# A state-space and MLP block on one core: group 1 turned by VectorE and transfers, not by TensorE

## The chip, the cores and the metric

The kernel runs on one core of a Trainium2 chip. The metric is the device time of one execution in microseconds; lower is better. The engines are named as in the profile: PE (TensorE; PEld is its weight load), DVE (VectorE), ACT (ScalarE), POOL (GpSimd), SP (SyncE, which here only issues transfers).

## The reference

All data is float32. The input `x` has 2048 tokens of 512 channels. A layer norm and a long convolution per channel (a state-space filter of 128 modes) give `h`; then a mixer and an MLP follow:

```python
h = x + conv(_layernorm(x))
z = _layernorm(h)
a = _gelu(_layernorm(z) @ w1)          # layer 1, 512 -> 512
hs = shifted(a) @ w2                   # layer 2: quarters of the channels shifted by +1, -1, +2, -2 tokens
x1 = z + hs
out = h + x1 + _gelu(_layernorm(x1) @ w3) @ w4   # layers 3 and 4, 512 -> 1792 -> 512
```

## The kernel before

`conv_phase` computes `h` under a planner that orders its operations by cost and due time. `mixer_phase` follows; there the order on each engine is that in which the Python code calls the operations (the class `InOrder` keeps it for PE, DVE, ACT and POOL). SP takes its transfers in program order too, and a transfer that waits holds back those behind it.

The tokens are kept as 16 tiles of 128, `h[:, j, :]`, in four groups of four tiles: group q has tiles 4q to 4q+3. The mixer takes group 3 first, then 0, 1 and 2. A matrix product is made of three products of float32r parts (`PROD`): high by high, high by low, low by high. So each operand is split into a high part (a copy on ACT) and a low part (a subtraction on DVE).

What happens to a group ahead of layer 1:

- `finish(q)`: bn_stats and bn_aggr of its tiles on DVE, in `conv_phase`. It can be called for some tiles at a time (`early` is the first two, `late` the other two).
- `root([q])`: twelve small DVE operations on the group's means and variances, which give the scale and the offset.
- `norm1(q)`, line 1214: the normalized tiles are written to a quarter each of a buffer `XQ[...]` (group 1 to `XQ[2]`), by DVE (tensor_scalar) or by ACT (activation), after the condition in line 1218.
- the turn, which brings channels onto the partitions. There are two ways. `turn1(q)` (line 1224) calls `transposed`: 16 TensorE transposes against `ident` into four PSUM banks, and `split` makes the high and low parts from there. `swap` (line 1227) takes four DVE transposes, each of one tile in 32x32 blocks, into a second buffer, and then 16 transfers of 32 partitions by 2 KB that carry the blocks back to where they belong; `parts` makes the high and low parts from the buffer. Each transfer reads blocks that all four transposes wrote. `swap` can be given an order of the tiles and a list of queues, which the transfers take in turn by `b`.

Before the change, groups 3, 0 and 1 go by `turn1` and group 2 by `swap` on SP's queue. The swaps of the later layer norm (`turn2`) use SP's queue, one of them SP's and ACT's.

`layer1(q, f)` (line 1246) makes one of four blocks of 128 outputs for a group: 12 matmuls into a PSUM bank out of four, then two gelus on ACT, a subtraction on DVE, and for some tiles the wrap copies on POOL, which layer 2 needs at the ends of the sequence. For (3, 0) the 12 products are re-sorted, so that high parts come first. `layer2(j)` makes one tile: 12 matmuls into a bank of the same four, then DVE adds (`scalar_tensor_tensor`), and for the first eight tiles POOL adds it to `h` (`residual`) and DVE takes its statistics. The order around the change is written out by hand in lines 1422 to 1431. `raw3`, `raw4` load weights on SP's queue, and `sum3` adds some of them on POOL.

The functions that the change touches, and what calls them:

Of the kernel before, what the change touches and what calls it, by code (L numbers as in the profile page):

```python
# [292 lines left out]
def norms(nc, cst, qs):  # L293

    ra, rb, rr, nb = cst["norm"]
    mv, t = cst["mv"], slice(qs[0] * 4, qs[-1] * 4 + 4)
    return [
        lambda: nc.vector.tensor_scalar(ra[:, 0, t], mv[:, t, 1], EPS, None, ALU.add),
        lambda: nc.vector.tensor_scalar(ra[:, 1, t], mv[:, t, 1], 1.0 + EPS, EPS * EPS, ALU.mult, ALU.add),
        *rsqrt_ops(nc, None, None, rr[:, :, t], ra[:, :, t], rb[:, :, t]),  # L300
        lambda: nc.vector.scalar_tensor_tensor(
            nb[:, :, t], mv[:, t, 0].unsqueeze(1).to_broadcast([128, 2, len(qs) * 4]), -1.0, rr[:, :, t], ALU.mult, ALU.mult),
    ]
# [825 lines left out]
def mixer_phase(ctx, tc, cst, h, out, finish, w3, w4):  # L1129

    nc = InOrder(tc)
# [10 lines left out]
    def slab(name):  # L1142
        return sl.tile([128, 512], F32R, tag="slab", name=name)
# [7 lines left out]
    XQ = [w1p.tile([128, 4 * 512], F32, name=f"xq{i}") for i in range(4)]  # L1151
# [5 lines left out]
    def bank(name):  # L1157
        return ps.tile([128, 512], F32, tag="bank", name=name)
# [11 lines left out]
    def gelu(b, name):  # L1170

        hi, lo, g = slab(f"{name}h"), slab(f"{name}l"), tmp(f"g{name}")
        nc.scalar.activation(hi, b, AF.Gelu_apprx_tanh)
        nc.scalar.activation(g, b, AF.Gelu_apprx_tanh)
        nc.vector.tensor_tensor(lo, g, hi.bitcast(F32), ALU.subtract)
        return hi, lo
# [10 lines left out]
    def root(qs):  # L1187
        for op in norms(nc, cst, qs):
            op()

    def transposed(tiles, name, first=0):

        b = [wide_bank(c, f"{name}_{c}") for c in range(4)]

        def turn(i, c):
            nc.tensor.transpose(b[c][:, i * 128 : i * 128 + 128], tiles[i][:, c * 128 : c * 128 + 128], ident)

        for i in range(first):  # L1200
            for c in range(4):
                turn(i, c)
        res = []
        for c in range(4):
            for i in range(first, 4):
                turn(i, c)
            res.append(split(b[c], f"{name}{c}"))
        return res
# [3 lines left out]
    H1, XL, XT = {}, {}, {}  # L1212

    def norm1(q):
        XL[q] = []
        for j in range(q * 4, q * 4 + 4):
            t = quarter(XQ[{3: 0, 0: 1, 1: 2, 2: 0}[q]], j % 4)
            if (q == 0 and j % 2) or (q == 3 and j != 14):
                nc.vector.tensor_scalar(t, h[:, j, :], mv[:, j, 0:1], r12[:, j : j + 1], ALU.subtract, ALU.mult)
            else:  # L1220
                nc.scalar.activation(t, h[:, j, :], AF.Identity, scale=r12[:, j : j + 1], bias=off12[:, j : j + 1])
            XL[q].append(t)

    def turn1(q):
        XT[q] = transposed(XL.pop(q), f"xt{q}", 2 if q == 3 else 0)

    def swap(x, t, order=range(4), queues=(nc.sync,), between=lambda: None):

        blocks = t.rearrange("p (b c i t) -> p i c b t", b=4, c=4, i=4)
        for i in order:  # L1230
            nc.vector.transpose(blocks[:, i], quarter(x, i).rearrange("p (c b t) -> p c b t", c=4, b=4))
        between()
        for a in range(4):
            for b in range(4):
                queues[b % len(queues)].dma_start(quarter(x, a)[b * 32 : b * 32 + 32], quarter(t, b)[a * 32 : a * 32 + 32])
        return [turned(x)[:, c] for c in range(4)]

    def parts(src, name, low=nc.vector):

        hi, lo = slab(f"{name}h"), slab(f"{name}l")  # L1240
        src = src.rearrange("p a (i t) -> p i a t", i=4)
        nc.scalar.copy(natural(hi), src)
        low.tensor_tensor(natural(lo), src, natural(hi).bitcast(F32), ALU.subtract)
        return hi, lo

    def layer1(q, f):
        b = bank(f"l1_{q}_{f}")
        n = 0
        seq = [(c, wi, xi) for c in range(4) for wi, xi in PROD]
        if (q, f) == (3, 0):  # L1250

            seq.sort(key=lambda k: 2 * k[0] + 3 * k[2])
        for c, wi, xi in seq:
            nc.tensor.matmul(b, W1[f][wi][:, c * 128 : c * 128 + 128], XT[q][c][xi], start=(n == 0), stop=(n == 11))
            n += 1
        H1[q, f] = gelu(b, f"h1_{q}_{f}")

        tiles = {0: ((15, 0),), 2: ((14, 1), (15, 2)), 1: ((0, 3),), 3: ((0, 4), (1, 5))}[f]
        for t, i in tiles:
            if t // 4 != q:  # L1260
                continue
            for k in range(2):
                src = H1[q, f][k][:, t % 4 * 128 : t % 4 * 128 + 128]
                dst = wrap[k][i // 4][:, i % 4, :]
                if f in (0, 2):
                    nc.gpsimd.tensor_copy(dst[:, 32:128], src[:, 0:96].bitcast(F32))
                    nc.gpsimd.tensor_copy(dst[:, 1:32], src[:, 96:127].bitcast(F32))
                    nc.gpsimd.tensor_copy(dst[:, 0:1], zero)
                else:
                    nc.gpsimd.tensor_copy(dst[:, 0:96], src[:, 32:128].bitcast(F32))  # L1270
                    nc.gpsimd.tensor_copy(dst[:, 96:127], src[:, 1:32].bitcast(F32))
                    nc.gpsimd.tensor_copy(dst[:, 127:128], zero)
# [3 lines left out]
    def h1_block(f, j, k):  # L1276
        if 0 <= j < 16:
            return H1[j // 4, f][k][:, j % 4 * 128 : j % 4 * 128 + 128]
        return wrap[k][WRAP[f, j] // 4][:, WRAP[f, j] % 4, :]
# [4 lines left out]
    def layer2(j):  # L1284
        q, i = divmod(j, 4)
        b = bank(f"l2_{j}")
        n = 0
        for f, sh in enumerate((-1, 1, -2, 2)):
            for wi, xi in PROD:
                nc.tensor.matmul(b, h1_block(f, j + sh, xi), W2[f][wi], start=(n == 0), stop=(n == 11))  # L1290
                n += 1
        x1 = quarter(X1[q], i)
        nc.vector.scalar_tensor_tensor(x1, h[:, j, :], r1[:, j : j + 1], b, ALU.mult, ALU.add)
        xq[j] = x1
        if j < 8:
            residual(j), stats2(j)

    def residual(j):
        (nc.gpsimd if j < 12 else nc.vector).tensor_tensor(h[:, j, :], h[:, j, :], xq[j], ALU.add)

    def stats2(j):
        q, i = divmod(j, 4)
        if q not in mv2:
            mv2[q] = sm.tile([128, 4, 2], F32, tag="mv2", name=f"mv2_{q}")
        st = sm.tile([128, 6], F32, tag="bst", name=f"st1_{j}")
        nc.vector.bn_stats(st, xq[j])
        nc.vector.bn_aggr(mv2[q][:, i, :], st)
# [62 lines left out]
    def raw3(s):  # L1370
        f = s % half
        for i in range(2):
            o = (f + i * half) * 128
            nc.sync.dma_start(raw["ab"[i]].rearrange("p (c f) -> p c f", c=4),
                              w3[:, o : o + 128].rearrange("(c p) f -> p c f", p=128))

    def sum3():
        a11, a12, a21, a22 = (raw[n][:, i * 256 : i * 256 + 256] for n in "ab" for i in range(2))
        s1, s2, s3, s4 = (raw["s"][:, i * 256 : i * 256 + 256] for i in range(4))
        nc.gpsimd.tensor_tensor(s1, a21, a22, ALU.add)  # L1380
        nc.gpsimd.tensor_tensor(s3, a11, a21, ALU.subtract)
        nc.gpsimd.tensor_tensor(s2, s1, a11, ALU.subtract)
        nc.gpsimd.tensor_tensor(s4, a12, s2, ALU.subtract)
# [16 lines left out]
    def raw4(s):  # L1400
        for i in range(2):
            f = s % half + i * half
            nc.sync.dma_start(raw["45"[i]], w4[f * 128 : f * 128 + 128, :])
# [15 lines left out]

    gelus = lambda: nc.scalar.activation(zero, zero, AF.Gelu_apprx_tanh)  # L1420
    early, late = range(2), range(2, 4)
    norm1(3), finish(0, early), turn1(3), gelus(), finish(0, late), root([0]), norm1(0)
    layer1(3, 0), layer1(3, 1), layer1(3, 2), turn1(0), finish(1), root([1]), layer1(3, 3), norm1(1), raw3(0), raw4(0)
    finish(2, early), layer1(0, 0), layer1(0, 1), layer1(0, 2), layer1(0, 3), turn1(1), finish(2, late), root([2]), layer2(0), layer2(1)
    norm1(2), sum3()
    third = swap(XQ[0], XQ[1])
    layer1(1, 0), layer1(1, 1), layer1(1, 2), layer1(1, 3), load3(0), raw3(1)
# [123 lines left out]
    for s in range(2 * half):  # L1551
# [27 lines left out]
        late = layer3b(s)  # L1579
# [56 lines left out]
```

## Time and profile before

| | us |
|---|---|
| median of 3 runs | 690.6 |
| lowest and highest run | 689.83, 692.06 |
| the profiled execution | 690.04 |
| its span, first to last instruction | 688.0 |
| PE busy | 651.1 |
| DVE, ACT, POOL busy | 543.0, 409.3, 398.5 |

A line of the timeline gives the start in us from the span's start, the length, the engine, the line of the code, the operation, the tile written and those read, the shapes and the count; in brackets stands how long the engine was idle before it and whose work ended that. Operations that follow one another overlap a little, so a cost is read from one start to the next. `SPq` and `ACTq` are the issues of transfers on those queues. A line of the chain of waits has start, length and what it is; every instruction is at line 87, the helper that keeps the order, so that the tiles' names tell them apart: `xt` are the turned inputs (xt10h: group 1, first 128 channels, high part), `l` the banks of layers 1 and 2, `h_0l` a low part of layer 1's output, `xq` the buffers.

### The profile page before, as it was taken

To read this page: it belongs to the slowest core of one execution; us is meant where nothing else is said; L and a number is where in the kernel's file an instruction comes from. 1 tells how busy PE (TensorE), PEld (TensorE's weight loads), DVE (VectorE), ACT (ScalarE), POOL (GpSimd) and SP (SyncE) were. 2 spreads that over 40 slices of the span, in tenths; PEclk is the share of its full clock that TensorE was granted. 3 is DMA by queue.
4 is the path that set the end of the run, shared out by engine and by line. 5 is a ranking of instruction groups with operands and counts; after the bars stand their busy time and mean duration, and the time that the engine had idled before them with its cause. 6 is when DMAs were issued, how large, how long until landed. Compare 5 with 4: busy or idle time off the path is not lost.

```text
span 688.0 us, 16756 instructions
## 1 busy us (share of the span) xinstructions
PE 651.1 (95%) x6822; PEld 507.7 (74%) x6822; DVE 543.0 (79%) x954; ACT 409.3 (59%) x708; POOL 398.5 (58%) x406
## 2 busy tenths in 40 slices
PE   5887989998999997989999999999999999999997
PEld 5884756663677684748888888888888888888886
DVE  5998898999898998988868799766879954454554
ACT  7889778867889975245734455544465543444330
POOL 1889589967999998002456209355635555554210
PEclk9998999999999999999999999999999999999999
DMA  8830644011201133010032311133311342211004
GB/s 216 258 145 2 194 153 104 3 48 32 64 3 50 33 111 93 2 61 1 1 92 74 82 30 38 55 90 99 104 46 40 103 132 62 62 46 47 18 13 123
DMA packets 48752, 50.43 MB, mean 73 GB/s; under 512 B 6180, under 2 KB 32804, under 8 KB 48676
## 3 DMA queue, kind: packets, MB, share of 16 engines
q1 hardware_dynamic: 47524, 47.80, 24.5%
q10 hardware_dynamic: 1152, 1.57, 0.9%
q8 instruction: 53, 0.87, 0.5%
q14 instruction: 23, 0.19, 0.1%
HBM read 35.72 MB, written 8.39 MB: 64 GB/s over the span
## 4 chain that ended last, share of the span: by engine, by line
PE 62%; DVE 14%; ACT 11%; POOL 4%; DMA 4%; issue 3%; SPq 1%; DVEq 0%; ACTq 0%; POOLq 0%
PE l L87 24%; PE acc L87 11%; PE bank L87 7%; ACT pt L87 7%; DVE u L87 4%; DVE at L87 3%; PE l3e L87 3%; PE l3c L87 3%; PE l3g L87 3%; PE l3f L87 3%; PE l3b L87 3%; PE l3a L87 3%; PE l3d L87 3%; DMA h<-in_A_u_dram 3%; DVE cs L87 2%
## 5 line engine op out<-in xcount | busy, mean ns | idle before, releaser
L87 ACT ACTIVATE pt<-pt 128x1056 f32<-128x1056 int32 x64 | 70.0, 1094 | 14.6 <-DVE cs L87 6.6
L87 POOL TENSOR_TENSOR pt<-p,s 128x512 int32<-128x512 int32 x64 | 72.2, 1146 | 4.5 <-DVE sn L87 3.6
L87 PE MATMUL bank<-at,tbs 128*64 128x128 f32 (+1 forms) x768 | 63.1, 311 | 3.4 <-DVE u L87 1.6
L87 PEld LDWEIGHTS bank<-at,tbs 128*64 128x64 f32 x768 | 44.6, 134 | 20.6 <-ACT at L87 2.9
L87 PEld LDWEIGHTS bank<-ident 128*128 128x128 f32 x418 | 49.9, 196 | 8.3 <-issue 5.1
L87 PE MATMUL bank<-ident 128*128 128x128 f32 x418 | 54.0, 285 | 0.0
L87 PE MATMUL bank<-u,ms 64*128 64x128 f32 x768 | 50.5, 280 | 3.5 <-DVE at L87 1.3
L87 PEld LDWEIGHTS bank<-u,ms 64*128 64x128 f32 x768 | 45.3, 187 | 8.3 <-issue 1.8
L87 POOL TENSOR_TENSOR cs0w<-raw,cs0w 128x512 fp32r<-128x512 f32 x7 | 9.1, 1297 | 58.9 <-ACT cs0w L87 47.3
L87 DVE TENSOR_TENSOR cs<-pt,amx 128x512 f32<-128x512 f32 x64 | 41.1, 682 | 2.4 <-ACT pt L87 1.2
L87 PEld LDWEIGHTS bank<-cs 128*32 128x32 f32 x1024 | 24.1, 111 | 22.5 <-POOL cs L87 6.0
L87 PE MATMUL bank<-cs 128*32 128x64 f32 x1024 | 32.4, 224 | 8.6 <-DVE cs L87 4.4
L87 DVE TENSOR_TENSOR h<-h,l 128x512 f32<-128x512 f32 x48 | 32.0, 685 | 10.6 <-PE l L87 10.6
L87 POOL TENSOR_TENSOR sn1w<-raw,sn1w 128x512 fp32r<-128x512 f32 x7 | 9.5, 1363 | 53.3 <-ACT sn1w L87 50.5
L87 ACT COPY at<-bank 128x512 f32<-128x512 f32 x40 | 24.9, 630 | 23.2 <-PE bank L87 23.1
L87 DVE TENSOR_TENSOR u<-u,l3f 128x512 f32<-128x512 f32 x14 | 9.6, 682 | 36.9 <-PE l3f L87 36.9
L87 ACT ACTIVATE pt<-pt,halfpi 128x1056 f32<-128x1056 f32 x32 | 38.2, 1192 | 0.5
L87 POOL TENSOR_TENSOR sn<-pt,amp 128x512 f32<-128x512 f32 x30 | 36.7, 1222 | 1.4 <-ACT pt L87 1.0
L87 DVE STREAM_TRANSPOSE at<-bank 128x512 f32<-128x512 f32 (+1 forms) x40 | 35.8, 930 | 1.9 <-PE bank L87 1.9
L87 ACT ACTIVATE u<-u 128x512 f32<-128x512 f32 x56 | 35.4, 633 | 1.8
L87 PE MATMUL bank<-sn 128*32 128x64 f32 x1024 | 31.9, 222 | 2.7 <-DVE sn L87 2.4
L87 POOL TENSOR_TENSOR cs<-pt,amp 128x512 f32<-128x512 f32 x26 | 31.8, 1223 | 3.6 <-PE bank L87 1.2
(1160 smaller groups left out, 2077.6 us busy)
## 6 DMA issues: line engine op xcount, KB each, us to landing
raw<-in_B_w_dram SPq DMA_DIRECT2D x28, 256.0 KB, 2.8
xq<-xq SPq DMA_DIRECT2D x72, 64.0 KB, 2.0
h<-in_A_u_dram SPq DMA_DIRECT2D x32, 128.0 KB, 4.2
h<-in_A_u_dram SPq DMA_DIRECT2D x16, 256.0 KB, 4.1
rawa<-in_B_w_dram SPq DMA_DIRECT2D x14, 256.0 KB, 2.8
rawb<-in_B_w_dram SPq DMA_DIRECT2D x14, 256.0 KB, 2.8
ms<-in_mm_dram SPq DMA_DIRECT2D x4, 768.0 KB, 11.2
out_dram<-h SPq DMA_DIRECT2D x48, 64.0 KB, 1.7
```

The source lines that it names most:

```text
L87: ins = f(*args, **kw)
```

## The change

Group 1 (tiles 4 to 7) is turned by `swap`, with its tiles in the order 1, 3, 0, 2 and its 16 transfers alternately on SP's queue and on GpSimd's; `turn1(1)` goes. `parts` of the result stands where `turn1(1)` stood. The first half of group 1's statistics moves ahead of layer 1 of group 3. `layer1(3, 3)` moves behind the normalization and the swap of group 1. In `norm1(1)`, two of the four tiles go to DVE. `layer1(1, 0)` takes its products in the re-sorted order.

```diff
-            if (q == 0 and j % 2) or (q == 3 and j != 14):
+            if (q < 2 and j % 2) or (q == 3 and j != 14):
...
-        if (q, f) == (3, 0):
+        if (q, f) in ((3, 0), (1, 0)):
...
-    norm1(3), finish(0, early), turn1(3), gelus(), finish(0, late), root([0]), norm1(0)
-    layer1(3, 0), layer1(3, 1), layer1(3, 2), turn1(0), finish(1), root([1]), layer1(3, 3), norm1(1), raw3(0), raw4(0)
-    finish(2, early), layer1(0, 0), layer1(0, 1), layer1(0, 2), layer1(0, 3), turn1(1), finish(2, late), root([2]), layer2(0), layer2(1)
+    norm1(3), finish(0, early), turn1(3), gelus(), finish(0, late), root([0]), norm1(0), finish(1, early)
+    layer1(3, 0), layer1(3, 1), layer1(3, 2), turn1(0), finish(1, late), root([1]), norm1(1), raw3(0), raw4(0)
+    second = swap(XQ[2], XQ[1], (1, 3, 0, 2), (nc.sync, nc.gpsimd))
+    layer1(3, 3), finish(2, early), layer1(0, 0), layer1(0, 1), layer1(0, 2), layer1(0, 3), finish(2, late)
+    XT[1] = [parts(v, f"xt1{c}") for c, v in enumerate(second)]
+    root([2]), layer2(0), layer2(1)
     norm1(2), sum3()
     third = swap(XQ[0], XQ[1])
```

## The prediction

> **What bounds the kernel now.** I read the page first (busy times, then the chain that ended last), then the chain in order of time, then each engine's timeline around the edit. On the page PE is busy for 95% of the span and carries most of the chain:
>
> ```profile
> PE 651.1 (95%) x6822; PEld 507.7 (74%) x6822; DVE 543.0 (79%) x954; ACT 409.3 (59%) x708; POOL 398.5 (58%) x406
> PE 62%; DVE 14%; ACT 11%; POOL 4%; DMA 4%; issue 3%; SPq 1%; DVEq 0%; ACTq 0%; POOLq 0%
> ```
>
> That is an average over stages, so the chain in order of time says more (start, length, what):
>
> ```profile
> 304.50 1.30 PE xt L87 x10
> 306.52 8.60 PE l L87 x36
> 315.12 1.75 PE xt L87 x16
> 316.87 13.65 PE l L87 x60
> 330.52 1.75 PE xt L87 x16
> 332.26 65.52 PE l L87 x288
> ```
>
> From 306.5 us on there are only PE pieces, end to end: the mixer is bound by PE, and every other engine hides behind it. The three "xt" pieces are the TensorE turns of groups 3, 0 and 1. The third is what the change takes out. So a gain can only be that piece, and a loss can only be PE made to wait.
>
> **What goes: PE's turn of group 1.**
>
> ```profile
> 330.13 0.39 PE L87 MATMUL l<-xt03h,sn0w 128*128 128x512 f32 x1
> 330.36 1.91 PE L87 MATMUL xt<-ident,xq 128*128 128x128 f32 x16
> 332.02 0.71 PE L87 MATMUL l<-sn0w,wrap 128*128 128x512 f32 x2
> 337.56 0.39 PE L87 MATMUL l<-xt10h,cs0w 128*128 128x512 f32 x1
> ```
>
> By starts, 332.02 - 330.36 = **1.66 us** leave PE. Then layer2(0) follows layer1(0,3) directly and needs its low part ten matmuls later. The trace has this meeting already, at layer1(1,3) and layer2(2):
>
> ```profile
> 348.21 0.39 PE L87 MATMUL l<-xt13h,sn0w 128*128 128x512 f32 x1
> 350.71 0.39 PE L87 MATMUL l<-amp0w,h_3l 128*128 128x512 f32 x1
> 349.76 0.69 DVE L87 TENSOR_TENSOR h_3l<-gh,h_3h 128x512 fp32r<-128x512 f32 x1 [2.03 <-ACT gh L87]
> ```
>
> The low part is ready at 350.45, and 350.71 follows its predecessor without a gap. I cost this new wait at nothing; without that cover (VectorE late) it costs what VectorE is late. PE then wants group 1's turned input at 337.56 - 1.66 = 335.90.
>
> **What comes: VectorE's part.**
>
> ```profile
> 303.86 1.46 DVE L87 TENSOR_SCALAR xq<-h,mvh,rr 128x512 f32<-128x512 f32 x3
> 315.37 0.71 DVE L87 TENSOR_TENSOR h_0l<-gh,h_0h 128x512 fp32r<-128x512 f32 x1 [1.64 <-ACT gh L87]
> 320.32 2.46 DVE L87 BATCH_NORM_STATS2 bs<-h 128x6 f32<-128x512 f32 x4
> 323.10 0.24 DVE L87 TENSOR_SCALAR ra<-mvh 128x4 f32<-128x4 f32 x2
> 325.28 0.69 DVE L87 TENSOR_TENSOR h_3l<-gh,h_3h 128x512 fp32r<-128x512 f32 x1
> 335.29 1.28 DVE L87 BATCH_NORM_STATS2 bs<-h 128x6 f32<-128x512 f32 x2
> 336.82 0.24 DVE L87 TENSOR_SCALAR ra<-mvh 128x4 f32<-128x4 f32 x2
> 339.00 0.74 DVE L87 SCALAR_TENSOR_TENSOR xq<-h,rr,l 128x512 f32<-128x512 f32 x1
> 342.18 2.46 DVE L87 STREAM_TRANSPOSE xq<-xq 128x512 f32<-128x512 f32 x4
> 325.40 2.94 ACT L87 ACTIVATE xq<-h,rn,rr 128x512 f32<-128x512 f32 x4 [4.64 <-DVE rn L87]
> ```
>
> Two tiles' statistics cost 336.82 - 335.29 = 1.53. The early pair falls into the 1.64 us in which DVE waits ahead of 315.37: hidden. If that cover is gone, group 3's low parts come up to 1.5 us later, and PE asks for their wrap copies only in layer2(0), some 10 us on. From 320.32: the late pair 1.53, the root 2.18 (323.10 to 325.28), so it ends at 324.0 and no longer at 325.28; two normalizations at 1.46 / 3 = 0.49, end at 325.0. ACT makes the other two tiles from 324.0 at 2.94 / 4 = 0.74, done at 325.5, before their turns come (order 1, 3, 0, 2). Four transposes at 2.46 / 4 = 0.62: **327.5**. Behind them DVE has h_3l of group 3, two statistics and group 0's low parts: about 2.1 us up to 329.6, then four times 0.6, so the last meets its ACT input near 331.7. On ACT the gelu of layer1(3,3) now stands behind the normalization, until about 326.5; PE wants its bank for layer1(0,3) about 12 matmuls (2.7 us) ahead of 330.36, at 327.6. Both cost nothing, with about 0.4 and 1.1 us to spare.
>
> **The transfers.** All sixteen wait for the four transposes, since each reads blocks of all four.
>
> ```profile
> 344.72 10.12 SPq L1235 DMA_DIRECT2D xq<-xq  x16
> 384.56 4.68 ACTq L87 DMA_DIRECT2D xq<-xq  x7
> 356.41 0.62 ACT L87 CAST xt20h<-xq 128x512 fp32r<-128x512 f32 x1 [4.92 <-DMA xq<-xq]
> 357.06 0.69 DVE L87 TENSOR_TENSOR xt20l<-xq,xt20h 128x512 fp32r<-128x512 f32 x1 [1.25 <-ACT xt20h L87]
> 339.82 1.29 POOL L87 TENSOR_TENSOR h<-h,xq 128x512 f32<-128x512 f32 x1 [5.26 <-DVE xq L87]
> ```
>
> SP issues in 10.12 / 16 = 0.63 us, and ACT's copy starts 356.41 - 354.84 = 1.6 us after the last issue ended. So SP's eight are usable at 327.5 + 5.1 + 1.6 = 334.2, in time. GpSimd issues no transfer in this trace. Bounds for one issue there: 0.63 (SP; ACT has 4.68 / 7 = 0.67) and 1.29, POOL's own pass over 128x512. No row is nearer, and I take the middle, about **1.0**. Then the copy can start at T = 327.5 + 8.0 + 1.6 = 337.1 (334.2 at 0.63; 339.4 at 1.29). The Trainium skill (DMA: Bandwidth & Descriptors, Latency and other measured facts) gives 1 us to the first byte from GpSimd against 0.6 from SP; scaled on SP's row that is an estimate of 1.05 an issue, and the sum below would come to 692.0.
>
> Queued behind these waits: on POOL the wrap copies, a residual and sum3, none wanted by PE soon; on SP nothing before the third group's transfers; on ACT norm1(2); on DVE the low parts, root([2]) and layer2(0)'s eviction. That last one matters.
>
> **The sum.** PE's layer1(1,0) starts when the first copy is done, T + 0.7 = 337.8, and its re-sorted order follows the low parts with about 0.1 lost: PE stands at T + 0.8 - 337.56 = **+0.3**, 2.0 us of waiting against 1.66 gained. Next late is the third group. Its chain runs root([2]), evictions, transposes, transfers, all on DVE behind the low parts. Four low parts take some 2.4 us from T + 0.65, so root([2]) starts at T + 3.06 = 340.2 instead of 336.82: 3.4 late. Before, the third group's first low part was ready at 357.06 + 0.69 = 357.75 and wanted here:
>
> ```profile
> 359.58 0.39 PE L87 MATMUL l<-xt20l,cs0w 128*128 128x512 f32 x1
> ```
>
> 1.83 us of slack. It is 3.4 - 0.3 = 3.0 late against PE, so PE stalls **1.2** more. The bank that layer1(1,2) takes over from layer2(0) is free at T + 6.0 and wanted at T + 6.2: nothing. In all T - 335.6 = **+1.5**: 690.04 + 1.5 = **691.6** in the profiled execution's own time (span 688.0 plus 2.04 around it). The median, 690.6, lies 0.6 above that execution; the range takes this in. What follows is paced by PE and moves with it.
>
> **Rivals.**
>
> *Hidden* (0.20). GpSimd issues as fast as SP and ACT do here. T = 334.2, PE doesn't wait, and 1.66 are gained; the third group is 0.4 late, 2.1 against PE, which costs 0.2. 690.04 - 1.4 = 688.6. For: both other queues lie at 0.63 to 0.67. Break-even is T = 335.6, 0.81 an issue. 1.66 caps the gain.
>
> *A slow GpSimd issue* (0.18). Above 1.07 an issue, or a first issue that costs extra, the loss passes 2.07 us; at 1.29 it is 3.8: 693.9. For: on 128x512 POOL takes 1.29 where DVE takes 0.69.
>
> *VectorE in GpSimd's way* (0.12). Slower, with its place: the eight issues run beside five low parts of DVE at 0.66. DVE and POOL do lengthen each other:
>
> ```profile
> 343.35 0.73 POOL L87 TENSOR_TENSOR raws<-rawa,rawb 128x256 f32<-128x256 f32 x1
> 344.87 1.07 POOL L87 TENSOR_TENSOR raws<-rawa,raws 128x256 f32<-128x256 f32 x1
> 345.26 1.23 DVE L87 TENSOR_TENSOR h_1l<-gh,h_1h 128x512 fp32r<-128x512 f32 x1
> ```
>
> The same POOL operation takes 0.73 beside transposes and 1.07 beside low parts, and DVE's 0.69 becomes 1.23. If an issue stops for each, T moves by 5 x 0.66 = 3.3, to 340.4: +4.8, 694.9. It decides from 0.1 us lost per issue (at which +1.5 passes 2.07). Against: an issue needn't read what DVE reads. The Trainium skill (SBUF — State Buffer, the "DVE blocks DMA" trap) says that VectorE's two-port operations, such as tensor_scalar, keep GpSimd from writing its descriptors; in this kernel the large ones end before the transposes, so by that rule nothing is added.
>
> *Two queues land no sooner than one* (0.06): the change doesn't do what it says. T = 327.5 + 10.1 + 1.6 = 339.2, +3.6, 693.7. Against: sixteen of them with other loads left the DMA engines at 0.43:
>
> ```profile
> 348.00:360.00 12.00, 12.00 (x54) 9.94 (x53) 6.82 (x14) 5.03 (x9) 6.84 (x5) 1.00 0.43 114
> ```
>
> **How the numbers follow.** The forecast, 0.81 to 1.07 an issue with PE waiting a little, has 0.44 and its own range is 690.0 to 692.1. What a measurement of this kernel can tell from no change is about 0.3%, 2.07 us. Slower by more: 0.18 + 0.12 + 0.06, and 0.02 of the forecast's edge, 0.38. Faster by more: the cap of 1.66 rules it out but for the scatter of the runs, 0.04 out of the hidden case. Same: 0.58. The range reaches from near the hidden case to the contention case, 688.8 to 694.8.
>
> **What would show it.** Transposes ending near 327.5; POOL's eight issues in some 8 us; a PE gap of about 2 us ahead of layer1(1,0), put down to ACT's first copy and behind it a DMA; a second gap of about 1 us at layer1(2,0), with root([2]) near 340. Wrong if POOL's issues take 5 us (no gap), or if the transposes end late, because statistics, root or normalization didn't move forward by the 1.3 us that I count on.

## The result, and the profile after

| | before | after |
|---|---|---|
| median, us | 690.67 (22 runs) | 692.3 (22 runs) |
| lowest to highest | 689.78 to 692.06 | 691.24 to 693.52 |
| the profiled execution | 690.04 | 692.15 |
| its span | 688.0 | 690.3 |

The ratio is 1.0024 [1.0018, 1.0031]: 1.6 us slower by the medians, a small loss (the interval lies above 1) within the 0.3% that the prediction called "same". 691.6 was forecast for the profiled execution; it took 692.15. That the number is so close is luck: two of its terms were wrong in opposite directions, as the stages show.

The page of after, busy times and shares of the chain that ended last:

```profile
PE 651.8 (94%) x6806; PEld 506.9 (73%) x6806; DVE 546.7 (79%) x960; ACT 407.8 (59%) x706; POOL 401.5 (58%) x414
PE 57%; DVE 15%; ACT 12%; POOL 5%; DMA 4%; issue 4%; SPq 2%; ACTq 0%; DVEq 0%; POOLq 0%
```

PE has 16 instructions fewer, yet its share of the chain fell from 62% to 57%: elsewhere something ends last that did not before. (PE's busy sum, with modelled ends, doesn't show the 1.66 us that went.) Where, the chain of after in order of time says:

```profile
307.25 8.60 PE l L87 x36
...
317.60 30.25 PE l L87 x132
...
356.27 1.99 DMA xq<-xq
...
358.44 0.63 ACT xt20h L87
...
359.09 0.69 DVE xt20l L87
...
363.70 2.94 ACT xq L87 x4
...
368.39 2.40 DVE xq L87 x4
...
373.39 1.14 DVE h_3l L87
...
374.58 25.23 PE l L87 x110
```

Before, the chain was one run of PE from 306.5 us on. Now it leaves PE at 317.60 + 30.25 = 347.85 for 26.7 us: the third group's transfers, its first copy on ACT (358.44) and low part on DVE (359.09), norm2(0) (363.70), four transposes (368.39) and the low parts of layer1(2, f), h_3l the last of them; PE takes over again at 374.58.

The first line also shows 0.73 us lost ahead of the edit: layer 1 begins at 307.25 and no longer at 306.52, in a part whose code is the same. Over all kernels below this start lies anywhere from 306.1 to 308.7. So I compare the **stage**, from layer 1's first matmul to layer 3's first. These are its ends, in before and in after:

```profile
306.52 0.73 PE L87 MATMUL l<-xt30h,cs0w 128*128 128x512 f32 x2
397.62 0.39 PE L87 MATMUL l3a<-b1100h,ptw 128*128 128x512 f32 x1
```

```profile
307.25 0.73 PE L87 MATMUL l<-xt30h,cs0w 128*128 128x512 f32 x2
399.64 0.39 PE L87 MATMUL l3a<-b1100h,ptw 128*128 128x512 f32 x1
```

The stage is 91.10 us before and 92.39 after: **+1.29**. Inside it, first the new turn, in after's timeline:

```profile
325.67 2.48 DVE L87 STREAM_TRANSPOSE xq<-xq 128x512 f32<-128x512 f32 x4
328.18 5.45 SPq L1235 DMA_DIRECT2D xq<-xq  x8
328.46 4.18 POOL L87 DMA_DIRECT2D xq<-xq  x8 [8.07 <-DVE xq L87]
335.90 0.62 ACT L87 CAST xt10h<-xq 128x512 fp32r<-128x512 f32 x1 [3.53 <-DMA xq<-xq]
336.33 0.39 PE L87 MATMUL l<-ptw,h_3h 128*128 128x512 f32 x1
336.57 0.73 PE L87 MATMUL l<-xt10h,cs0w 128*128 128x512 f32 x2
338.97 0.24 DVE L87 TENSOR_SCALAR ra<-mvh 128x4 f32<-128x4 f32 x2
```

GpSimd issues in 4.18 / 8 = 0.52 us, faster than SP (5.45 / 8 = 0.68). PE goes from layer2(1) into layer1(1,0) without a gap (336.33 to 336.57); the copy is done at 336.52, just in time. With the 0.73 taken off, that start is 335.84 against 337.56: all of the turn's time is gained, 1.72. Then the third group:

```profile
359.11 0.50 PE L87 MATMUL l<-xt20h,cs0w 128*128 128x512 f32 x1 [0.30 <-ACT xt20h L87]
359.84 0.50 PE L87 MATMUL l<-xt20l,cs0w 128*128 128x512 f32 x1 [0.22 <-DVE xt20l L87]
```

PE waits at both, and is then only 0.47 ahead of before (359.84 - 0.73 against 359.58). And last, layer2(6), after:

```profile
370.71 1.53 DVE L87 TENSOR_TENSOR h_1l<-gh,h_1h 128x512 fp32r<-128x512 f32 x1
372.17 1.22 DVE L87 TENSOR_TENSOR h_2l<-gh,h_2h 128x512 fp32r<-128x512 f32 x1
373.31 1.21 DVE L87 TENSOR_TENSOR h_3l<-gh,h_3h 128x512 fp32r<-128x512 f32 x1
372.70 0.39 PE L87 MATMUL l<-amp0w,h_3h 128*128 128x512 f32 x1
374.58 0.50 PE L87 MATMUL l<-amp0w,h_3l 128*128 128x512 f32 x1 [1.49 <-DVE h_3l L87]
```

and the same place before:

```profile
368.67 1.54 DVE L87 TENSOR_TENSOR h_1l<-gh,h_1h 128x512 fp32r<-128x512 f32 x1
370.13 1.23 DVE L87 TENSOR_TENSOR h_2l<-gh,h_2h 128x512 fp32r<-128x512 f32 x1
371.55 0.94 DVE L87 TENSOR_TENSOR h_3l<-gh,h_3h 128x512 fp32r<-128x512 f32 x1 [0.20 <-ACT gh L87]
372.27 0.39 PE L87 MATMUL l<-amp0w,h_3h 128*128 128x512 f32 x1
372.55 0.50 PE L87 MATMUL l<-amp0w,h_3l 128*128 128x512 f32 x1
```

Matmuls here follow each other in 0.23 us. Before, the low part h_3l was done at 372.49 and its matmul started at 372.55, 0.05 late: no slack on PE's side. DVE itself stood idle for only 0.20 ahead of h_3l, waiting for ACT's gelu. After, it starts 1.88 after its predecessor: a wait of 1.65. DVE comes 2.03 later in this trace from xt20l (357.06, then 359.09) to h_1l (368.67, then 370.71) and hands that on undiminished. With the 0.73 taken off it is 1.30, and that is what the stage loses.

So the stage's account: -1.72 for the turn, +0.21 in layer1(1,0) with its low parts (the next block starts at 339.50, before at 340.28), +1.04 up to the first low part of layer1(2,0) (0.95 of it the two waits there), +0.17 of small gaps, +1.60 at layer2(6), which is the 1.29 (with 0.01 of rounding).

### The profile page after: what moved, and what is told of

The parts are those of the page before. It is cut to its first block, busy times and chain, and to the rows that moved or that the text cites. A ratio compares the mean times of both kernels' runs of the same rounds, so it can differ in the third digit from the quotient of the medians.

```text
span 690.3 us, 16773 instructions
## 1 busy us (share of the span) xinstructions
PE 651.8 (94%) x6806; PEld 506.9 (73%) x6806; DVE 546.7 (79%) x960; ACT 407.8 (59%) x706; POOL 401.5 (58%) x414
## 4 chain that ended last, share of the span: by engine, by line
PE 57%; DVE 15%; ACT 12%; POOL 5%; DMA 4%; issue 4%; SPq 2%; ACTq 0%; DVEq 0%; POOLq 0%
PE l L87 20%; PE acc L87 11%; ACT pt L87 7%; PE bank L87 6%; DVE u L87 3%; DVE at L87 3%; PE l3e L87 3%; PE l3a L87 3%; PE l3c L87 3%; PE l3g L87 3%; PE l3f L87 3%; PE l3b L87 3%; PE l3d L87 3%; DVE cs L87 2%; DVE sn L87 2%
```

## The experiments

Each ratio is to the kernel before in the same set of runs. Two theories were to be told apart at first. **A**: the loss is the third group's chain, late because root([2]) stands on DVE behind low parts that wait for transfers. **B**: GpSimd's transfers themselves cost it, by late landing or by what they hold up. A was later narrowed to **A2**: the lateness becomes time at layer2(6), since there DVE's low parts run beside GpSimd's work and had next to no slack before.

**1. root([2]) ahead of the low parts**

```diff
+    root([2])
     XT[1] = [parts(v, f"xt1{c}") for c, v in enumerate(second)]
-    root([2]), layer2(0), layer2(1)
+    layer2(0), layer2(1)
```

> The changed kernel with root([2]) moved ahead of group 1's high and low parts. Theory A (the loss is the third group's chain: root([2]) waits on VectorE behind low parts that wait 2.05 us for the transfers): root([2]) fills that wait, the third group's first copy starts about 2.1 us earlier against PE, the waits at layer1(2,0) (0.45 and 0.5 us) go, and of the 1.65 us at layer2(6) some 0.8 stay. So about 2 us faster than the changed kernel, 690.2, and 0.3 to 0.8 us faster than the kernel before. Theory B (the loss is GpSimd's transfers themselves, the wrap copies behind them and VectorE in GpSimd's way): no difference to the changed kernel, 692.3.

691.38, ratio 1.0006 [0.9993, 1.0019]; stage 91.64. About half of the 2 us that A said. PE's rows in this kernel:

```profile
338.76 0.50 PE L87 MATMUL l<-xt10l,cs0w 128*128 128x512 f32 x1 [0.91 <-DVE xt10l L87]
...
373.87 0.50 PE L87 MATMUL l<-amp0w,h_3l 128*128 128x512 f32 x1 [0.57 <-DVE h_3l L87]
```

The waits at layer1(2,0) are gone and the one at layer2(6) fell from 1.49 to 0.57, but the root now makes group 1's low parts late, 0.91. The lateness matters, as A says; this order only moves part of it.

**2. turn2(0) behind layer1(2,3)**

```diff
-    layer1(2, 0), turn2(0), layer1(2, 1), load4(0), raw4(1), layer1(2, 2), sum3(), layer1(2, 3), layer2(6)
+    layer1(2, 0), layer1(2, 1), load4(0), raw4(1), layer1(2, 2), sum3(), layer1(2, 3), turn2(0), layer2(6)
```

> The changed kernel with turn2(0) moved behind layer1(2,3), so that its four transposes no longer stand ahead of three low parts on VectorE. Theory A: the wait of 1.65 us at layer2(6) goes, 690.6; the later turn may give part or all of it back where its 16 transfers end some 4 us later and layer 3 or ACT waits for them. Theory B: no gain at layer2(6), 692.3 or more.

694.78, ratio 1.0056 [1.0035, 1.0077], 4.2 us above A's number. With the transposes away the stage is 91.23, but the waits of layers 2 and 3 show what was given back:

```profile
ACT b1100h L87 <- DMA xq<-xq: 3.8, 1, 3.8
...
PE l3b L87 <- DVE t200l L87: 1.4, 1, 1.4
...
PE l3e L87 <- DVE u L87: 0.8, 1, 0.8
```

Layer 3 gets its first operands late. The transposes do stand in layer2(6)'s way, but they can't go.

**3. The third swap on two queues too**

```diff
-    third = swap(XQ[0], XQ[1])
+    third = swap(XQ[0], XQ[1], range(4), (nc.sync, nc.gpsimd))
```

> The changed kernel with the third group's 16 transfers too alternately on SP's and GpSimd's queue. Theory A: the third group lands about 4.5 us earlier, PE waits neither at layer1(2,0) nor at layer2(6), and the 1.66 us of the turn remain as gain: 689.2, faster than the kernel before by 1.3 to 1.7. Theory B: more GpSimd issues, more loss: 693 or more.

691.9, ratio 1.0014 [1.0, 1.0028]; stage 91.85. A's number is missed by 2.7 us. The timeline of this kernel, DVE, POOL and PE:

```profile
354.76 3.32 DVE L87 TENSOR_TENSOR xt20l<-xq,xt20h 128x512 fp32r<-128x512 f32 x1 [0.96 <-DMA rawa<-in_B_w_dram]
...
346.74 3.93 POOL L87 DMA_DIRECT2D xq<-xq  x8
...
355.00 2.53 POOL L87 TENSOR_TENSOR h<-h,xq 128x512 f32<-128x512 f32 x2
...
372.86 0.50 PE L87 MATMUL l<-amp0w,h_3l 128*128 128x512 f32 x1 [1.52 <-DVE h_3l L87]
```

ACT's first copy, xt20h, starts some 4 us sooner (353.30 against 358.44, of which 1.16 is this run's earlier start), but the first low part takes 3.32 us instead of 0.69: it runs beside GpSimd's operations and ends only after its two residuals (355.00 + 2.53 = 357.53), 0.55 later. And the wait at layer2(6) is unchanged, with h_1l to h_3l still at 1.2 to 1.5. From here on GpSimd's neighbours are the suspect, and A becomes A2.

**4. The second swap on SP's queue alone**

```diff
-    second = swap(XQ[2], XQ[1], (1, 3, 0, 2), (nc.sync, nc.gpsimd))
+    second = swap(XQ[2], XQ[1], (1, 3, 0, 2))
```

> The changed kernel with group 1's 16 transfers all on SP's queue. Eight more issues at 0.63: the first copy at about 339.9 and not 335.9. Theory A: PE waits 4.0 us ahead of layer1(1,0), root([2]) and the third group move with it, so the waits behind it stay about as they are against PE: 692.3 + 4.0 = 696.3. Theory B: GpSimd's issues are gone and with them their cost, so the loss is under 3 us: below 695.

695.58, ratio 1.0069 [1.0045, 1.0093]; stage 96.42. PE waits at layer1(1,0):

```profile
341.70 1.22 PE L87 MATMUL l<-xt10h,cs0w 128*128 128x512 f32 x2 [3.83 <-ACT xt10h L87]
```

The time lies between A's 696.3 and B's 695, and its interval holds both; the stage decides: 4.03 longer than after's, the 4.0 that A said. GpSimd's queue is worth about 3 us in all (1.0069 against 1.0024). B falls: what GpSimd issues helps.

**5. load4 and sum3 away from layer2(6)** (after, with GpSimd's work behind turn2(1) and layer2(7))

```diff
-    layer1(2, 0), turn2(0), layer1(2, 1), load4(0), raw4(1), layer1(2, 2), sum3(), layer1(2, 3), layer2(6)
-    layer2(7), norm2(1)
+    layer1(2, 0), turn2(0), layer1(2, 1), layer1(2, 2), layer1(2, 3), layer2(6)
+    layer2(7), sum3(), norm2(1)
...
-    layer2(8), turn2(1, (3, 0, 1, 2), (nc.sync, nc.scalar), first_splits)
+    layer2(8), turn2(1, (3, 0, 1, 2), (nc.sync, nc.scalar), first_splits), load4(0), raw4(1)
```

> The changed kernel with load4(0) and raw4(1) moved behind turn2(1) and sum3() behind layer2(7), so that GpSimd does nothing while VectorE makes the low parts of layer1(2, 1 to 3). Theory A2 (the third group comes about 1 us late against PE, and at layer2(6) the lateness turns into a wait because h_1l, h_2l, h_3l take 1.5, 1.2 and 1.2 us beside GpSimd's work instead of 0.6 each): the low parts take 0.6 to 0.7, the wait of 1.65 us at layer2(6) goes, the two of 0.45 and 0.5 at layer1(2,0) stay: 692.3 - 1.6 = 690.7. Rival A (the lateness alone, no matter what GpSimd does): transposes still stand ahead of the low parts, at most 0.3 gained, 692.0.

693.53, ratio 1.0047 [1.0035, 1.006]. The time is missed by 2.8 us, the mechanism is not: the stage is 90.54, 1.85 less than after's, and the low parts are short:

```profile
370.21 0.65 DVE L87 TENSOR_TENSOR h_1l<-gh,h_1h 128x512 fp32r<-128x512 f32 x1
...
371.49 0.69 DVE L87 TENSOR_TENSOR h_3l<-gh,h_3h 128x512 fp32r<-128x512 f32 x1
```

PE has no wait there. But layer 3 has the waits of experiment 2 again (l3b 1.4, l3e 0.8).

**6. Experiments 3 and 5 together**

> Both: the third group's transfers on SP's and GpSimd's queue, and the GpSimd work of the run before moved away. Theory A2: of the waits on PE behind the turn only some 0.5 us at layer1(2,0) stays (xt20l held up by GpSimd's load3 and residual work), so 691.9 - 1.5 = 690.4, and counted from the first matmul of layer 1 some 0.8 us less than the kernel before. Rival A: 691.6 to 691.9.

693.8, ratio 1.0049 [1.0037, 1.0062]; stage 89.76, and the same loss at layer 3, so that 690.4 is missed by 3.4 us.

**7. The move of experiment 5 in the kernel before**

> The kernel before with the same GpSimd work moved away, as a control. It waits 0.1 to 0.3 us at layer2(6), so both theories expect no more than that: 690.4 to 690.8.

694.7, ratio 1.0061 [1.0048, 1.0074]; missed by 4 us. So the loss at layer 3 belongs to the move and not to the swap. Its timeline shows two sources, on DVE, POOL and ACT:

```profile
380.01 0.66 DVE L87 TENSOR_SCALAR qr<-qb 128x4 int32<-128x4 int32 x1
...
379.91 0.74 POOL L87 TENSOR_TENSOR raws<-rawa,rawb 128x256 f32<-128x256 f32 x1
...
383.28 0.55 DVE L87 TENSOR_SCALAR xq<-xq,qr,qo 128x512 f32<-128x512 f32 x1
...
392.29 1.14 ACT L87 CAST cs0w<-raw 128x512 fp32r<-128x512 f32 x2 [4.72 <-DMA xq<-xq]
...
394.41 2.20 DVE L87 TENSOR_TENSOR sn0w<-raws,cs1w 128x1024 fp32r<-128x1024 f32 x1 [5.58 <-ACT cs1w L87]
```

sum3 now falls on the root of norm2(1), whose operations take up to 0.66 where they took 0.17, so that its normalization starts at 383.28: 1.75 later than before (380.29), with the 1.24 taken off by which this run's layer 1 began later. load4's copies on ACT (392.29) then hold back the one of a layer 3 weight, cs1w, by 1.05, and DVE's subtraction of that weight, beside load4's on GpSimd, takes 2.20 instead of 1.23. DVE's first sum for layer 3 behind it starts at 396.54, before at 391.51: 3.79 late by the same reckoning, 1.75 from sum3's move and 2.0 from load4's. This is read from the rows; no run moves one of the two alone. Beside this kernel, experiment 5 has the shorter stage, 90.54 against 90.94, and a median 1.2 us lower, though the intervals overlap: under the same move, the swap seems to gain.

**8. All of the change but the swap** (turn1(1) stays; early statistics, two tiles on DVE, the re-sorted order, layer1(3,3) later)

> The kernel before with every edit of the change but the swap: earlier statistics, half of norm1(1) on VectorE, layer1(3,3) behind it, re-sorted layer1(1,0); group 1 is still turned by TensorE. If these edits cost nothing by themselves (as the prediction has it): 690.7 within 0.3. If part of the loss is theirs: 691.5 or more.

690.31, ratio 1.0005 [0.9996, 1.0014]; stage 91.08. As expected, by the ratio: these parts cost and gain nothing.

**9. sum3 beside turn2(0)'s transposes, load4 behind layer1(2,3)** (after)

```diff
-    layer1(2, 0), turn2(0), layer1(2, 1), load4(0), raw4(1), layer1(2, 2), sum3(), layer1(2, 3), layer2(6)
+    layer1(2, 0), turn2(0), sum3(), layer1(2, 1), layer1(2, 2), layer1(2, 3), load4(0), layer2(6)
...
-    layer2(8), turn2(1, (3, 0, 1, 2), (nc.sync, nc.scalar), first_splits)
+    layer2(8), turn2(1, (3, 0, 1, 2), (nc.sync, nc.scalar), first_splits), raw4(1)
```

> The changed kernel with the same GpSimd work in other places: sum3() ahead of layer1(2,1), where it falls beside turn2(0)'s transposes, load4(0) behind layer1(2,3), raw4(1) behind turn2(1). Theory A2 (GpSimd's work beside two-input operations of VectorE turns the third group's lateness into the wait at layer2(6); the 4 us that the earlier attempt lost came from the same thing at norm2(1)'s root): low parts of 0.6 to 0.7, no wait at layer2(6), no loss at layer 3. From layer 1's first matmul to layer 3's 90.5 us as in that attempt (the kernel before 91.1, the changed one 92.4), so 690.1 to 690.5 in all. Rival A (the lateness alone): 692.

690.5, ratio 0.9999 [0.9991, 1.0008]; stage 90.58. As expected, 1.8 us under after, with nothing lost at layer 3. Its timeline, DVE and POOL:

```profile
368.96 2.48 DVE L87 STREAM_TRANSPOSE xq<-xq 128x512 f32<-128x512 f32 x4
371.37 0.65 DVE L87 TENSOR_TENSOR h_1l<-gh,h_1h 128x512 fp32r<-128x512 f32 x1
...
369.60 0.74 POOL L87 TENSOR_TENSOR raws<-raws,rawa 128x256 f32<-128x256 f32 x1
...
373.02 1.35 POOL L87 TENSOR_TENSOR cs0w<-raw,cs0w 128x512 fp32r<-128x512 f32 x1 [1.86 <-ACT cs0w L87]
```

In these rows, beside transposes, neither engine is lengthened; load4 comes when the low parts are all but through.

**10. Experiments 3 and 9 together**

> The same with the third group's transfers too on SP's and GpSimd's queue. Theory A2: 89.8 us from layer 1's first matmul to layer 3's, 1.3 us less than the kernel before, which would be 689.3 to 689.7. Rival A: 691.5.

690.19, ratio 0.9987 [0.9978, 0.9997]; stage 89.80, 1.30 under before. The stage is as expected, the median 0.5 above the 689.3 to 689.7 that were. It is the only version whose interval lies below the kernel before, by 0.7 us in the medians of its set. One wait is left of the two at layer1(2,0):

```profile
358.39 0.50 PE L87 MATMUL l<-xt20l,cs0w 128*128 128x512 f32 x1 [0.37 <-DVE xt20l L87]
```

**11. The move of experiment 9 in the kernel before**

> The control: the kernel before with the GpSimd work moved likewise. It has at most 0.3 us of wait to lose at layer2(6): 690.3 to 690.7 by both theories. Above that the new places cost something by themselves.

690.54, ratio 1.0001 [0.999, 1.0013]; stage 90.97. As expected: without the swap the move brings nothing, though it gives DVE room:

```profile
371.45 0.69 DVE L87 TENSOR_TENSOR h_3l<-gh,h_3h 128x512 fp32r<-128x512 f32 x1 [1.49 <-ACT gh L87]
```

**12. layer1(1,0) in its plain order** (after)

```diff
-        if (q, f) in ((3, 0), (1, 0)):
+        if (q, f) == (3, 0):
```

> The changed kernel with layer1(1,0) in its plain order. PE must wait some 0.4 us for the first low part there. Theory A2: PE waits for VectorE's chain later anyway (layer1(2,0), layer2(6)), and that chain does not hang on PE, so the time does not move: 692.3 within 0.3. If the time of PE's own work counted here, 692.7.

692.06, ratio 1.0024 [1.0013, 1.0034]; stage 92.34. layer1(1,0) takes PE 3.37 us (336.64 to 340.01), 0.44 more than in after (336.57 to 339.50), and yet stage and time are those of after: between there and layer2(6) PE isn't the bound, as A2 says.

The four kernels that decide it, by stage in us and ratio to before (the medians come from different sets):

| | GpSimd's work as it was | moved (9, 11) |
|---|---|---|
| TensorE turn | 91.10, 1 | 90.97, 1.0001 |
| swap of group 1 | 92.39, 1.0024 | 90.58, 0.9999 |

Neither the swap nor GpSimd's work beside the low parts alone accounts for the loss at layer2(6). Before, the contention used up nearly all the slack there: DVE's idle time ahead of h_3l is 0.20, and 1.49 with GpSimd's work moved (11). The swap's lateness then came on top. Each stage is one profile, but kernels that differ little in it agree within 0.05: before and experiment 8 (91.10, 91.08), after and 12 (92.39, 92.34), 9 and 5 (90.58, 90.54), 10 and 6 (89.80, 89.76), 11 and 7 (90.97, 90.94).

## Why the prediction came out as it did

- **PE loses 1.66 us.** Right: 1.72 ahead at layer1(1,0).
- **VectorE's part ends at 327.5.** Right: 325.67 + 2.48 - 0.73 = 327.42. The early statistics and the later layer1(3,3) are hidden (experiment 8), and the new meeting with layer2(0) costs nothing.
- **POOL issues in about 1.0 us** ("I take the middle"). Wrong: 0.52, below the stated lower bound of 0.63. What ends last is SP's half, 328.18 + 5.45 = 333.63, and ACT's first copy 2.27 after that (1.6 was taken). T is 335.90 - 0.73 = 335.2 and not 337.1, so PE's 2.0 us of waiting at layer1(1,0) didn't come. This is the prediction's own sign of being wrong, issues in 5 us and no gap. The rule that the prediction cited beside it, the Trainium skill (DMA: Bandwidth & Descriptors, Latency and other measured facts), agrees with the trace in the direction of the landing alone, a median of 2.8 us from GpSimd against 2.0 from SP; scaled to the issue it pointed the wrong way:

```profile
xq<-xq SPq DMA_DIRECT2D x80, 64.0 KB, 2.0
xq<-xq POOLq DMA_DIRECT2D x8, 64.0 KB, 2.8
```

- **The third group is next late, 1.2 us.** Right in mechanism and nearly in size: root([2]) starts behind the low parts, at 338.97 - 0.73 = 338.24 instead of 336.82, and PE loses 1.04 at layer1(2,0). The prediction had root at 340.2; the error cancels, because a sooner T moves PE as well.
- **"What follows is paced by PE and moves with it."** This is the step that failed. By the prediction's own sum, T - 335.6, the measured T gives -0.4: a small gain, 689.6 in all. PE is indeed 0.47 ahead at layer1(2,0), so the sum is right up to there. The stage lost 1.29. The difference of 1.7 is, but for 0.1, the wait at layer2(6) (1.60). DVE's low parts there were as late as PE could bear already: two chains were critical at once, one of PE and one of DVE (with ACT and the transfers). Taking work off PE alone could hardly have gained beyond that point, since DVE had only its 0.20 to give; that is worked out from the rows, and no run tests it. The rows of before had it (h_3l done at 372.49, its matmul at 372.55, 0.05 late); the prediction compared times only at the next meeting, layer1(2,0).
- **The rivals.** *Hidden* was right about the place (no wait of note at layer1(1,0)) and wrong about the gain. By the prediction's own break-even, 0.81 an issue, it is the case that came, with 0.52, and it had a chance of 0.20. *A slow GpSimd issue*: no. *Two queues no sooner than one*: no; experiment 4 shows what one queue costs, and its T, 341.03 less the 1.91 by which that run began later, is 339.1, as that rival had it (339.2). *VectorE in GpSimd's way* was wrong on transfers: the five low parts of DVE beside the eight issues keep 0.65 to 0.69. But the same two engines did decide the result, 40 us later, between arithmetic instructions.

That contention is in the rows: beside GpSimd's additions and subtractions a low part takes 0.77 to 1.54, in the three kernels with the third swap on two queues 3.2 to 3.3, alone 0.65 to 0.69. It looks like waiting for one another, not like both running slower: in after, GpSimd's operation of 370.40 ends at 371.70, h_1l 0.54 later at 372.24, and GpSimd's next one, begun at 371.65 and 0.74 long when alone, 0.60 after that, at 372.84. The Trainium skill (SBUF — State Buffer, Who interferes with whom) says that a VectorE instruction with two SBUF inputs contends with a GpSimd instruction that reads SBUF, and one with a single input doesn't outside the two-port modes. The low parts and the transposes agree with it. Whether the one-input operations of the root in experiment 7 (0.66 instead of 0.17) ran in such a mode, no row shows.

What stays open: experiment 10's stage gains 1.30 and its median 0.7, and the interval of its ratio, 0.2 to 1.5 us, allows both; and what layer 3 loses in experiments 2, 5, 6 and 7 was read from rows only, not tested.

## What to carry to other kernels

Work taken off the bounding engine gains only up to the next place where another engine's chain arrives with no slack: follow the late chain from meeting to meeting, comparing on each when the operand was ready with when its matmul could have started, until it has room again. Where such a place is tight, look at what GpSimd does beside VectorE's two-input instructions; moving that work beside transposes was worth more here, 1.8 us, than the change itself.

## What was not expected of the hardware

- GpSimd issued a transfer of 32 partitions by 2 KB in 0.52 us (0.49 in experiment 3: 3.93 / 8), less than SP's 0.63 to 0.68, though it landed 0.8 later.
- A 128x512 subtraction on DVE that started amid GpSimd's operations took 3.32 us instead of 0.69 (3.18 and 3.29 in experiments 6 and 10); it didn't get in between two of them.
- DVE operations of 128x4, one-input ones too, took up to 0.66 instead of 0.17 beside GpSimd additions of 0.74, whose own time didn't change.
